# Attention values in split heads: the high and low passes of the last key block as one matmul of 256 columns, the spare columns added afterwards

## Chip, cores, metric

One core of one Trainium2 chip. The metric is the time of one execution on the device in microseconds; several executions are timed and their median is given. The core's engines are named as in the profile: PE (TensorE, matmuls), PEld (its weight loads), DVE (VectorE), ACT (ScalarE), POOL (GpSimd) and SP (SyncE, which issues most transfers).

## What is computed

Windowed attention with a few sink keys, then a two-layer MLP on the joined heads:

```python
batch, n_heads, seq, head_dim = (4, 8, 768, 64)     # n_sink 4, window 128
scores = scale * np.matmul(q, k.transpose(0, 1, 3, 2))
keep = is_sink | in_window
scores = np.where(keep, scores, -1000000000.0)
...
a = a / (np.sum(a, axis=-1, keepdims=True) + 1e-09)
attn = np.matmul(a, v)
x = attn.transpose(0, 2, 1, 3).reshape(B * S, H * D)      # 3072 x 512
h = x @ w_in                                             # 512 x 2048
out = np.maximum(0.01 * h, h) @ w_out                    # 2048 x 512
```

## The kernel before

The work is cut into 8 units `u` (4 batches, two halves of 384 queries each), and each unit into 8 heads `h`, taken in pairs. A head has three query blocks `j` of 128. For each block `scores` (L306) makes the score tile in PSUM (tag `s`, one buffer), `softmax` (L319) masks it, takes the exponent and normalises it, and `tail` (L377) transposes it (L382), splits it into a high part (ACT, L393) and a low part (DVE, L395), and lets POOL put it into `pt` (L353). `pt` holds for each head the transposed weights of all key blocks, `pt[:, 0]` the high parts and `pt[:, 1]` the low ones, 768 columns apart. Each number is split into a high part, which is its cast to the type fp32r, and a low part, which is what the cast leaves; products of high with high, high with low and low with high are summed in PSUM.

`values` (L427) is the changed function. Units 0 and 1 take its native branch, which multiplies without a split. Units 2 to 7, 48 heads, take the split branch: the values of one head stand in 128 weight columns, 64 for the high part and 64 for the low part, so that one pass gives both halves in the two halves of the partitions of `out`, a PSUM tile of 512 columns (tag `v`, one buffer). Each key block (`segments`, L346) is passed twice, with the high and with the low part of `pt`, and adds into its own columns of the 384 queries. The last key block touches only the last 128 queries. A pass for the sink keys (`st`) ends the group. In a unit of even number that makes 4 passes of 256 columns, 2 of 128 and the sink pass (7), in one of odd number 2 of 128, 4 of 256, 2 of 128 and the sink pass (9). Then ACT copies one half of the partitions out of PSUM into `xf` (L460), and DVE adds the other half from PSUM (L461). After the odd head of a pair `emit_x` (L510) splits `xf` into `xh` (L513, ACT) and `xl` (L514, DVE or POOL), which the MLP of that unit reads later.

`mlp_stream` (L548) has for each unit and each of 16 column blocks 12 matmuls for the hidden tile `h` (L565, PSUM, one buffer), then ACT (L572), DVE (L573), ACT (L574) and DVE (L575) for its split parts `gh` and `gl`, and 9 matmuls into the three output tiles (L586). In units 2 to 5 of the MLP `check_weights` (L188) also reads weights over again (L193 on ACT, L195 on POOL, L197 on DVE).

The order of TensorE's instructions is the order in which the program issues them: the two streams are interleaved by hand, step by step. The order on ACT, DVE, POOL and SP is worked out by a scheduler that simulates the program while it is built, so an added instruction may also move others. Each engine works through its own list in order.

Of the kernel before, what the change touches and what calls it, by code (L numbers as in the profile page):

```python
# [9 lines left out]
F32 = mybir.dt.float32  # L10
# [4 lines left out]
ALU = mybir.AluOpType  # L15
# [5 lines left out]
P = 128  # L21
# [10 lines left out]
TU = T * P  # L32
# [89 lines left out]
def fast_path(ctx, tc, cpool, wz, qk, vu, vs, w_in, w_out, out, ident, lim, masks, tri, diag,  # L122
              negm, wmin, wmax):
    nc = tc.nc
# [12 lines left out]
    phase = {}  # L137
# [65 lines left out]
    def native_values(u, h):  # L203
        return NATP0 <= (u * H + h) // 2 < NATP
# [141 lines left out]
    def segments(half):  # L346
        if half:
            return (0, 0, P), (P, 0, 2 * P), (3 * P, P, 2 * P), (5 * P, 2 * P, P)
        return (0, 0, 2 * P), (2 * P, P, 2 * P), (4 * P, 2 * P, P)
# [77 lines left out]
    def values(u, h, pt, st, state):  # L427
        half = u % 2
        pair, odd = divmod(h, 2)
        q0 = 0 if half else P  # L430
        hp = slice(odd * D, (odd + 1) * D)
        lp = slice((1 - odd) * D, (2 - odd) * D)
        if native_values(u, h) and not odd:
            state["v"] = vraws.pop((u, h))
        vv, sv = state["v"]
        if native_values(u, h):
            if not odd:
                state["acc"] = ps_v.tile([P, 512], F32, tag="v", name=f"v{u}_{h}")
            out = state["acc"][hp, :]
            mms = [(vv[:, kb * P + odd * D:kb * P + (odd + 1) * D], pt[:, 0, po:po + m], qo, m)  # L440
                   for kb, (po, qo, m) in enumerate(segments(half))]
            mms.append((sv[0:st.shape[0], hp], st, q0, TU - q0))
        else:
            out = ps_v.tile([P, 512], F32, tag="v", name=f"v{u}_{h}")
            cs = slice(odd * P, (odd + 1) * P)
            mms = [(vv[:, kb, cs], pt[:, c, po:po + m], qo, m)
                   for kb, (po, qo, m) in enumerate(segments(half)) for c in range(2)]
            mms.append((sv[:, 0, cs], st, q0, TU - q0))
        for c, (l, r, o, m) in enumerate(mms):
            nc.tensor.matmul(out[:, o:o + m], lhsT=l, rhs=r, start=c == 0, stop=c == len(mms) - 1,  # L450
                             skip_group_check=True)
            if u == 0 and c % PIECE == PIECE - 1 and c < len(mms) - 1:
                yield
        if native_values(u, h):
            x = state["acc"][:, 0:TU]
        else:
            if not odd:
                state["xf"] = xpool.tile([P, TU], F32, tag="xf", name=f"xf{u}_{pair}")
            x = state["xf"]
            nc.scalar.copy(out=x[hp, :], in_=out[lp, 0:TU])  # L460
            nc.vector.tensor_tensor(out=x[hp, :], in0=out[hp, 0:TU], in1=x[hp, :], op=ALU.add)  # L461
        if odd:
            vfree[pair % 2] = True
            emit_x(u, pair, x)

    def attend(u, h, pend, state):
# [34 lines left out]
        if odd:  # L501
            def gather():
                state["st"] = sinks(u, h // 2, sk)
                if u == 0 and h < H - 1:
                    load_weights(h // 2)
            pend.append(gather)
            for o in range(2):
                pend.append(lambda o=o: values(u, h - 1 + o, state["pt", o], state["st"], state))

    def emit_x(u, pair, x):  # L510
        xh = xpool.tile([P, TU], F32R, tag=f"xh{pair}", name=f"xh{u}_{pair}")
        xl = xpool.tile([P, TU], F32R, tag=f"xl{pair}", name=f"xl{u}_{pair}")
        nc.scalar.copy(out=xh, in_=x)  # L513
        (nc.gpsimd if u < XLP and not native_values(u, 2 * pair) else nc.vector).tensor_tensor(out=xl, in0=x, in1=xh.bitcast(F32), op=ALU.subtract)  # L514
        xs[u].append((xh, xl))
# [313 lines left out]
```

## Time and profile before

| | |
|---|---|
| median of 3 runs | 748.33 us (747.74 to 749.93) |
| profiled execution | 746.79 us, span 744.9 us |
| PE busy | 718.6 us (96%) |
| PEld busy | 623.4 us (84%) |
| DVE busy | 562.3 us (75%) |
| ACT busy | 434.3 us (58%) |
| POOL busy | 381.2 us (51%) |
| split value passes (L450) | from 174.1 to 656.2 us |

The profile is of one execution; times in it are microseconds from the start of its span. Matmuls overlap: one of 0.28 us may be followed by the next after 0.12, so what one costs is read from start to start. A "releaser" is what an engine waited for last.

### The profile page before, as it was taken

The page shows a single profiled execution, that of the slowest core. Times are in us where ns is not written, and L with a number is a line of the kernel's source. Part 1 is how long each engine was busy: PE and PEld are TensorE (multiplying, and loading weights), DVE is VectorE, ACT ScalarE, POOL GpSimd, SP SyncE. Part 2 cuts the span into 40 slices and gives each one's busy share as a digit, 9 for nine tenths or more (in the row PEclk, how much of TensorE's full clock was granted, in tenths as well). Part 3 has the DMA queues.
Part 4 walks back from the last instruction along what each step waited for, and adds up shares of the span by engine and source line. Part 5 has one row for each costly group of instructions (what it writes and reads, how often), then busy time and mean ns, then how long its engine had stood idle before and what let it go on. Part 6 is the DMA issues. An engine that isn't in the chain of part 4 may idle for free.

```text
span 744.9 us, 12686 instructions
## 1 busy us (share of the span) xinstructions
PE 718.6 (96%) x3935; PEld 623.4 (84%) x3935; DVE 562.3 (75%) x1832; ACT 434.3 (58%) x1208; POOL 381.2 (51%) x490
## 2 busy tenths in 40 slices
PE   8879999989999999999999999999999999999995
PEld 4547777769999988999988988999988999988985
DVE  6876889877667888888888888888888977733222
ACT  4667667657666566666566666666666655522221
POOL 3554456555445677665666577665666556300000
PEclk9989999999999999999999999999999999999998
DMA  5543566643212343324333443325331321001001
GB/s 179 181 151 119 186 205 185 190 136 100 58 55 64 115 125 122 90 93 152 114 108 106 133 125 112 96 93 157 114 107 48 106 69 43 1 1 42 1 1 46
DMA packets 30475, 76.94 MB, mean 103 GB/s; under 512 B 3585, under 2 KB 9153, under 8 KB 30401
## 3 DMA queue, kind: packets, MB, share of 16 engines
q1 hardware_dynamic: 30256, 75.94, 32.6%
q8 instruction: 33, 0.54, 0.3%
q14 instruction: 42, 0.34, 0.1%
q10 hardware_dynamic: 144, 0.13, 0.1%
HBM read 69.76 MB, written 6.29 MB: 102 GB/s over the span
## 4 chain that ended last, share of the span: by engine, by line
PE 84%; DVE 9%; ACT 3%; issue 2%; DMA 1%; POOL 0%; SPq 0%; ACTq 0%; DVEq 0%
PE o L586 32%; PE h L565 32%; PE v L450 10%; PE s L314 5%; PE t L382 2%; DVE gl L575 2%; PE warm L304 1%; PE t L369 1%; DVE pk L344 1%; DVE zeroi L197 1%; DMA woraw<-in_w_out 1%; ACT qksp L271 1%; DVE g L573 1%; DVE pk L334 0%; DVE xf L461 0%
## 5 line engine op out<-in xcount | busy, mean ns | idle before, releaser
L565 PE MATMUL h<-xh,wih 128*128 128x384 f32 x512 | 187.6, 366 | 1.4 <-DVE g L573 1.3
L565 PE MATMUL h<-xh,wil 128*128 128x384 f32 x512 | 172.7, 337 | 1.5 <-POOL wil L185 1.5
L565 PE MATMUL h<-xl,wih 128*128 128x384 f32 x512 | 172.3, 337 | 0.0
L586 PE MATMUL o<-woh,gh 128*128 128x512 f32 x384 | 154.2, 401 | 0.0
L586 PE MATMUL o<-woh,gl 128*128 128x512 f32 x384 | 151.3, 394 | 0.0
L586 PE MATMUL o<-wol,gh 128*128 128x512 f32 x384 | 151.2, 394 | 0.0
L353 POOL TENSOR_SCALAR_AFFINE_SELECT pt<-stg 128x256 fp32r<-128x256 f32 x240 | 101.4, 448 | 83.4 <-DVE stg L395 67.9
L272 POOL TENSOR_TENSOR qksp<-qkraw,qksp 64x524 fp32r<-64x524 f32 (+1 forms) x62 | 74.9, 1208 | 106.7 <-issue 61.7
L575 DVE TENSOR_TENSOR gl<-g,gh 128x384 fp32r<-128x384 f32 x128 | 105.6, 825 | 17.1 <-ACT gh L574 15.6
L573 DVE TENSOR_TENSOR g<-h,g 128x384 f32<-128x384 f32 x128 | 71.0, 555 | 60.5 <-ACT g L572 58.3
L565 PEld LDWEIGHTS h<-xh,wih 128*128 128x128 f32 x512 | 96.4, 188 | 15.9 <-issue 2.9
L572 ACT ACTIVATE g<-h 128x384 f32<-128x384 f32 x128 | 62.3, 487 | 69.9 <-PE h L565 69.3
L338 ACT ACTIVATE pk<-pk,negm 128x128 f32<-128x128 f32 (+2 forms) x168 | 70.3, 418 | 53.3 <-DVE negm L334 52.4
L565 PEld LDWEIGHTS h<-xl,wih 128*128 128x128 f32 x512 | 96.8, 189 | 3.2
L565 PEld LDWEIGHTS h<-xh,wil 128*128 128x128 f32 x512 | 96.1, 188 | 1.8 <-POOL wil L185 1.8
L314 PEld LDWEIGHTS s<-qksp 128*128 128x128 f32 x372 | 68.5, 191 | 22.5 <-issue 10.6
L586 PEld LDWEIGHTS o<-woh,gl 128*128 128x128 f32 x384 | 72.0, 188 | 16.4 <-DVE gl L575 0.2
L314 PE MATMUL s<-qksp 128*128 128x260 f32 (+1 forms) x372 | 76.6, 288 | 9.2 <-DVE pk L344 5.4
L574 ACT CAST gh<-g 128x384 fp32r<-128x384 f32 x128 | 65.7, 513 | 32.8 <-DVE g L573 30.5
L586 PEld LDWEIGHTS o<-woh,gh 128*128 128x128 f32 x384 | 72.4, 189 | 11.2 <-issue 2.4
L586 PEld LDWEIGHTS o<-wol,gh 128*128 128x128 f32 x384 | 72.2, 188 | 6.5
L274 POOL TENSOR_TENSOR qksp<-qkraw,qksp 128x384 fp32r<-128x384 f32 x62 | 67.8, 1094 | 4.7
(124 smaller groups left out, 1220.4 us busy)
## 6 DMA issues: line engine op xcount, KB each, us to landing
qkraw<-in_qk SPq DMA_DIRECT2D x32, 454.0 KB, 4.1
qkraw<-in_qk SPq DMA_DIRECT2D x30, 388.0 KB, 3.2
wiraw<-in_w_in SPq DMA_DIRECT2D x16, 512.0 KB, 3.6
woraw<-in_w_out SPq DMA_DIRECT2D x16, 512.0 KB, 3.8
ciraw<-in_w_in SPq DMA_DIRECT2D x16, 512.0 KB, 3.5
coraw<-in_w_out SPq DMA_DIRECT2D x16, 512.0 KB, 3.6
out<-ob SPq DMA_DIRECT2D x23, 256.0 KB, 2.0
vraw<-in_vu SPq DMA_DIRECT2D x12, 256.0 KB, 2.7
```

Of the source, the lines that this page charges most:

```text
L272: nc.gpsimd.tensor_tensor(out=sp[D:P, TU:TU + n], in0=raw[D:P, TU:TU + n], in1=sp[D:P, TU:TU + n].bitcast(F32), op=ALU.subtract)
L274: nc.gpsimd.tensor_tensor(out=sp[:, TU + n:2 * TU + n], in0=raw[:, 0:TU], in1=sp[:, 0:TU].bitcast(F32), op=ALU.subtract)
L314: nc.tensor.matmul(ps[:, 0:kn], lhsT=sp[rows, off + j * P:off + (j + 1) * P], rhs=sp[rows, TU + k0:TU + k0 + kn], start=c == 0, stop=c == ...
L338: nc.scalar.activation(out=e, in_=e, func=AF.Exp, scale=-1.0, bias=neg, accum_out=sm)
L353: nc.gpsimd.affine_select(out=out, in_=src, pattern=([[0, x]] if x > 1 else []) + [[sign, P]], base=-1 if prev else 0, channel_multiplier= ...
L450: nc.tensor.matmul(out[:, o:o + m], lhsT=l, rhs=r, start=c == 0, stop=c == len(mms) - 1, skip_group_check=True)
L565: nc.tensor.matmul(ph[:, 0:TU], lhsT=w[:, cs], rhs=x, start=cc == 0 and c == 0, stop=cc == NCC - 1 and c == 2)
L572: nc.scalar.mul(g, ph[:, 0:TU], 0.01)
L573: anchor[0] = nc.vector.tensor_tensor(out=g, in0=ph[:, 0:TU], in1=g, op=ALU.max)
L574: nc.scalar.copy(out=gh, in_=g)
L575: (nc.gpsimd if u == 0 and fc % 4 < GLP else nc.vector).tensor_tensor(out=gl, in0=g, in1=gh.bitcast(F32), op=ALU.subtract)
L586: nc.tensor.matmul(po[t], lhsT=gg[:, tsl], rhs=w, start=f == 0 and c == 0, stop=f == NFC - 1 and c == 2)
```

## The change

In the split branch the last key block is taken out of the list, and its two passes (high and low part of `pt`, 128 columns each, into the same columns) become one pass over both parts, 256 columns side by side: the high part goes into the block's own columns, the low part into columns 384 to 511 of the same PSUM tile, which were not used. These spare columns are then added to the last 128 queries: ACT copies one half of their partitions into a new tile `more`, DVE adds the other half from PSUM to `xf`, and then `more`. The native branch is as before.

```diff
             out = ps_v.tile([P, 512], F32, tag="v", name=f"v{u}_{h}")
             cs = slice(odd * P, (odd + 1) * P)
-            mms = [(vv[:, kb, cs], pt[:, c, po:po + m], qo, m)
-                   for kb, (po, qo, m) in enumerate(segments(half)) for c in range(2)]
+            *segs, (po, qo, m) = segments(half)
+            mms = [(vv[:, kb, cs], pt[:, c, a:a + n], o, n)
+                   for kb, (a, o, n) in enumerate(segs) for c in range(2)]
+            mms.append((vv[:, len(segs), cs], pt[:, :, po:po + m], qo, 2 * m))
             mms.append((sv[:, 0, cs], st, q0, TU - q0))
         for c, (l, r, o, m) in enumerate(mms):
-            nc.tensor.matmul(out[:, o:o + m], lhsT=l, rhs=r, start=c == 0, stop=c == len(mms) - 1,
+            dst = out[:, o:o + m]
+            if len(r.shape) > 2:
+                dst = dst.rearrange("p (c q) -> p c q", c=2)
+            nc.tensor.matmul(dst, lhsT=l, rhs=r, start=c == 0, stop=c == len(mms) - 1,
                              skip_group_check=True)
...
             x = state["xf"]
+            more = phase["late"].tile([P, P], F32, tag="more", name=f"more{u}_{h}", bufs=1)
+            end = x[hp, TU - P:]
             nc.scalar.copy(out=x[hp, :], in_=out[lp, 0:TU])
+            nc.scalar.copy(out=more[hp, :], in_=out[lp, TU:])
             nc.vector.tensor_tensor(out=x[hp, :], in0=out[hp, 0:TU], in1=x[hp, :], op=ALU.add)
+            nc.vector.tensor_tensor(out=end, in0=out[hp, TU:], in1=end, op=ALU.add)
+            nc.vector.tensor_tensor(out=end, in0=end, in1=more[hp, :], op=ALU.add)
```

## Rows read from the trace of the kernel before

**Rows 1.** The page's first part: busy time of each engine, its share of the span and its instructions.

```profile
PE 718.6 (96%) x3935; PEld 623.4 (84%) x3935; DVE 562.3 (75%) x1832; ACT 434.3 (58%) x1208; POOL 381.2 (51%) x490
```

**Rows 2.** The table of stretches: from and to, length, busy time of PE, PEld, DVE, ACT and POOL with their instructions, then the granted clock of TensorE, the DMA share and GB/s.

```profile
175.00:250.00 75.00, 75.00 (x429) 68.20 (x428) 52.08 (x184) 48.55 (x140) 40.81 (x58) 1.00 0.20 58
250.00:600.00 350.00, 348.75 (x1982) 314.67 (x1981) 303.12 (x1011) 221.37 (x630) 225.97 (x299) 1.00 0.37 113
600.00:657.00 57.00, 56.80 (x328) 51.55 (x326) 41.86 (x149) 30.86 (x86) 26.74 (x46) 1.00 0.10 29
```

**Rows 3.** The list of TensorE's waits from 175 to 657 us, all of it: who waited for whom, us in total, times, longest.

```profile
PE v L450 <- DVE xf L461: 0.9, 3, 0.4
```

**Rows 4.** One value pass of an even unit (head 2 of unit 4) in order of time, engine PE: start, us, instruction, count. Each row joins the passes of one kind that were running at a chosen instant and begins with the first of them; so 363.12, 363.24, 363.30 and 363.41 are the starts of the last pass of 256 columns, of the two of 128 and of the sink pass.

```profile
363.12 0.45 PE L450 MATMUL v<-pt,vsp 128*128 128x256 f32 x3
...
363.24 0.33 PE L450 MATMUL v<-pt,vsp 128*128 128x128 f32 x2
...
363.30 0.27 PE L450 MATMUL v<-pt,vsp 128*128 128x128 f32 x1
363.41 0.33 PE L450 MATMUL v<-st,ssp 128*128 128x256 f32 x1
```

**Rows 5.** The same pass, order of time, weight loads (PEld).

```profile
363.24 0.19 PEld L450 LDWEIGHTS v<-pt,vsp 128*128 128x128 f32 x1
363.35 0.19 PEld L450 LDWEIGHTS v<-st,ssp 128*128 128x128 f32 x1
```

**Rows 6.** Groups of instructions by line and shape, ACT, whole span: busy us, mean ns of one | idle before them and its releaser.

```profile
L393 ACT CAST stg<-t 128x128 fp32r<-128x128 f32 x120 | 30.8, 257 | 42.7 <-PE t L382 27.6 <-POOL pt L353 13.7 <-POOL qksp L274 1.3
...
L460 ACT COPY xf<-v 64x384 f32<-64x384 f32 x48 | 22.8, 475 | 6.0 <-PE v L450 4.9
```

**Rows 7.** The same for DVE, from 175 to 657 us.

```profile
L575 DVE TENSOR_TENSOR gl<-g,gh 128x384 fp32r<-128x384 f32 x92 | 82.2, 894 | 6.3 <-ACT gh L574 4.9
...
L395 DVE TENSOR_TENSOR stg<-t,stg 128x128 fp32r<-128x128 f32 x116 | 33.1, 285 | 6.0 <-ACT stg L393 5.3
...
L461 DVE TENSOR_TENSOR xf<-v,xf 64x384 f32<-64x384 f32 x47 | 25.8, 548 | 12.7 <-ACT xf L460 12.6
```

**Rows 8.** DVE in order of time behind the value pass of an even head (its passes run from 299.75 to 301.01).

```profile
302.55 0.14 DVE L339 TENSOR_SCALAR sm<-sm 128x1 f32<-128x1 f32 x1
302.73 0.16 DVE L340 RECIPROCAL sm<-sm 128x1 f32<-128x1 f32 x1
...
303.33 0.54 DVE L461 TENSOR_TENSOR xf<-v,xf 64x384 f32<-64x384 f32 x1
303.80 0.27 DVE L395 TENSOR_TENSOR stg<-t,stg 128x128 fp32r<-128x128 f32 x1
```

**Rows 9.** ACT in order of time in the same place.

```profile
302.16 0.48 ACT L460 COPY xf<-v 64x384 f32<-64x384 f32 x1
```

**Rows 10.** PE in order of time: the first value pass of odd heads, of the first, the second and the last of the 14 handoffs in which it starts 0.14 to 0.18 us after L461's end, and (240.03) of the tightest of the ten others. In brackets, where there is one, the idle time before it and its releaser.

```profile
240.03 0.28 PE L450 MATMUL v<-pt,vsp 128*128 128x256 f32 x1
...
282.81 0.41 PE L450 MATMUL v<-pt,vsp 128*128 128x128 f32 x2 [0.36 <-DVE xf L461]
...
304.01 0.30 PE L450 MATMUL v<-pt,vsp 128*128 128x128 f32 x1
...
655.31 0.30 PE L450 MATMUL v<-pt,vsp 128*128 128x128 f32 x1 [0.20 <-DVE xf L461]
```

**Rows 11.** DVE in order of time: L461 of the even heads before three of those passes (that of the pass at 304.01 stands in rows 8).

```profile
238.78 0.54 DVE L461 TENSOR_TENSOR xf<-v,xf 64x384 f32<-64x384 f32 x1
...
282.13 0.54 DVE L461 TENSOR_TENSOR xf<-v,xf 64x384 f32<-64x384 f32 x1
...
654.61 0.55 DVE L461 TENSOR_TENSOR xf<-v,xf 64x384 f32<-64x384 f32 x1 [1.04 <-ACT xf L460]
```

**Rows 12.** DVE in order of time behind the value pass of an odd head; the last row is the L334 of the odd head with the least distance to the next score pass.

```profile
306.51 0.56 DVE L461 TENSOR_TENSOR xf<-v,xf 64x384 f32<-64x384 f32 x1 [0.65 <-ACT xf L460]
307.10 0.56 DVE L575 TENSOR_TENSOR gl<-g,gh 128x384 fp32r<-128x384 f32 x1
307.69 0.30 DVE L323 COPY_PREDICATED s<-tri,s 128x128 f32<-128x128 int8 x1
...
308.37 0.28 DVE L334 CUSTOM_DVE_ANT_0 pk<-s,mw 128x132 f32<-128x132 f32 x1
...
391.80 0.29 DVE L334 CUSTOM_DVE_ANT_0 pk<-s,mw 128x132 f32<-128x132 f32 x1
```

**Rows 13.** PE in order of time: the score passes that follow those two.

```profile
309.18 0.28 PE L314 MATMUL s<-qksp 128*128 128x260 f32 x1
...
392.46 0.28 PE L314 MATMUL s<-qksp 128*128 128x260 f32 x1
```

**Rows 14.** Order of time near 274 us, DVE (L573, which frees the tile `h`) and PE (the next pass into `h`).

```profile
273.50 0.56 DVE L573 TENSOR_TENSOR g<-h,g 128x384 f32<-128x384 f32 x1 [0.36 <-ACT g L572]
...
274.11 0.44 PE L565 MATMUL h<-xh,wih 128*128 128x384 f32 x1
```

**Rows 15.** Order of time, POOL and PE: the last L514 of unit 2 and the pass that reads its result.

```profile
243.52 1.23 POOL L514 TENSOR_TENSOR xl<-xf,xh 128x384 fp32r<-128x384 f32 x1
...
250.03 0.34 PE L565 MATMUL h<-xl,wih 128*128 128x384 f32 x1
```

**Rows 16.** The list of DVE's waits over the whole span, the row of L595 (columns as in rows 3).

```profile
DVE ob L595 <- ACT ob L593: 0.4, 1, 0.4
```

## The prediction

> **What bounds the kernel now.** I read first the shares of busy time [rows 1] and then the table of stretches [rows 2]. The changed code runs only for units 2 to 7, which is the stretch from 175 to 657 us: 48 heads, one value pass each. There the reader should see TensorE busy in 480.55 of 482 us at full granted clock, and VectorE busy in 397.06 of them (82%; 303.12 of 350, or 87%, between 250 and 600). So TensorE sets the pace, each nanosecond saved on it counts, and each delay that reaches it counts too; VectorE has 85 us to spare, but in order and in small pieces. The list of waits is third [rows 3]: the only wait that it puts to TensorE's account in this stretch is that of the value pass for the addition of L461, 0.9 us in 3 pieces. That is the place that the change lengthens.
>
> **What the change removes.** Per head, the two 128-column passes of the last key block become one of 256 columns with the same weights. In one value pass in order of time [rows 4] a 256-column pass takes 0.12 us from its start to that of the next (363.12 to 363.24), the two 128-column ones together 0.17 us (363.24 to 363.41): the first is followed after 0.06, the second after 0.11. The weight loads show why: they start 0.11 us apart [rows 5], so a pass of 0.06 us that follows such a load waits for the next one. One pass of 0.12 us in place of 0.17 saves 0.05 us, times 48 heads: 2.4 us. The new moving operand has a gap between its halves, which no row on TensorE shows. If the gap cost nothing and the weight load were the bound, one load interval is saved, 48 x 0.11 = 5.3 us; if it cost the difference, nothing is saved. I take 2.4, as the pass is nearest to the contiguous 256-column one.
>
> By the columns alone there would be no saving: at 0.12 us for 256 columns, two passes of 128 cost 0.06 each. The Trainium skill (TensorE: Matmul & The Clock Gate, Back-to-back issue gap) states such a rule: an isolated pass costs its columns plus a small constant, which as an estimate from its table leaves 3 ns per head, 0.1 us in all, and a sum of +7.8 us in place of +5.5. The trace speaks against it here, with its 0.17 us.
>
> **What the change adds.** Per head one ScalarE copy of 64x128 out of PSUM, one VectorE addition that reads PSUM and SBUF (64x128, "first addition" below) and one that reads SBUF alone (the second). ScalarE: the nearest row is the 128x128 cast of L393 at 257 ns [rows 6], so 48 x 0.26 = 12.3 us on an engine that is busy 63% of 250 to 600 (221.37 of 350) [rows 2]; it hides there, and costs TensorE something only where an addition waits for it. First addition: L395 has the same columns and the same kinds of operands, 285 ns; L461 with 384 columns takes 548, so 1.03 ns per column. Second addition: its nearest row is L575, two SBUF operands of 384 columns, whose mean is 894 ns against 548 for L461 with as many [rows 7]; cut by 256 columns at 1.03 ns the two give 0.28 to 0.63 us, and I take 0.28, as the L575 that stands right behind a value pass takes 0.56 us [rows 12]. Both depend on the instruction before them: a dependent VectorE instruction starts 0.04 us after the end of its forerunner (302.55 + 0.14, then 302.73) [rows 8]. So VectorE's queue grows by about 0.32 + 0.28 = 0.6 us per head, 29 us of its 85 spare. As a total it fits. What counts is what stands behind it in the queue.
>
> **Place one, from even head to odd head.** All value passes share one PSUM buffer. The pass of the odd head starts about 4 us after that of the even one and waits until L461 has read the buffer. For the even head ScalarE copies at 302.16 [rows 9], but L461 comes to its turn at 303.33, behind the softmax chain, and ends at 303.87 [rows 8]; the odd head's pass starts at 304.01, 0.14 us later, which is just the way from the release to the start [rows 10]. Of 24 such handoffs 14 have 0.14 to 0.18 us there: the first is 282.13 + 0.54 to 282.81, the last 654.61 + 0.55 to 655.31 [rows 10, 11]. The ten others have 0.7 us and more (the tightest 238.78 + 0.54 to 240.03) and absorb it. With the change the last PSUM read is the first addition, 0.32 us later. In the 14 tight ones TensorE pays that, less up to 0.03: 14 x 0.30 = 4.2 us. The ends are zero, if the scheduler now places L461 earlier, and 14 x 0.6 = 8.4, if it slips another operation in between. What is queued behind the wait on TensorE is its whole stream. The second addition does not hold the buffer.
>
> **Place two, behind the odd head's L461.** Here VectorE runs without a pause from 306.51 (L461, after an idle 0.65 us in which it waited for ScalarE) through L575, L323 and L514 to L334 at 308.37, which frees the one PSUM buffer of the scores [rows 12]; the next score pass starts at 309.18 [rows 13], 0.53 us after L334's end. A released TensorE pass can start 0.05 us after VectorE's end (273.50 + 0.56, then 274.11) [rows 14], so 0.48 us are free. In 15 of the 24 odd heads the distance is 0.37 to 0.58 us (the tightest 391.80 + 0.29 to 392.46), in the others 0.75 and more, or no score pass follows. The additions are issued ahead of L323 and L334 in the program and are ready sooner, so I expect them between: 0.6 us more against 0.29 to 0.50 free, worked out one by one 2.7 us in all. The ends: zero if they are put behind L334, and 15 x 0.55 = 8.3 if the copy delays them as well or the second is disturbed.
>
> **Place three.** Twice, from 259 to 274 and 428 to 443 us, VectorE has no pause at all, and TensorE already waits for L573 (the pass at 274.11 comes those 0.05 us behind L573's end, as a waiting pass does) [rows 14]. Most of the 1.2 us that a pair adds there arrives at TensorE: 0.5 us each after what place two has charged, 1.0 us in all (0 to 2).
>
> **Hidden.** The x tiles come 0.6 us later, and so do the casts of L513 and L514. The least time between such a result and its use is 5 us (L514 ends at 244.75, its use is at 250.03) [rows 15], so this costs nothing; without that cover it would be 0.6 us per unit. No transfer and no queue of SyncE or GpSimd is touched, other than that GpSimd's placements wait for L395, which moves with place one.
>
> **Sum.** -2.4 + 4.2 + 2.7 + 1.0 = +5.5 us. The profiled execution took 746.79 us (span 744.9 and 1.9 around it), 1.54 below the median of the three runs, 748.33; against its own time the sum gives 752.3, against the median 753.8, which I take.
>
> **The rivals.** (a) *One reader of the buffer at a time.* The copy of the spare columns reads the same PSUM buffer as L461, in other partitions. At the kernel's end L595 waits 0.4 us for L593 although the two only share a PSUM buffer and an output tile, in different columns [rows 16]. If such readers are ordered, L461 starts 0.26 us later wherever it waits for ScalarE, which is at all odd heads: 15 x 0.26 and about 1 us from the next ones, +5 on top, +10.5 or 758.8. The Trainium skill (PSUM — Partial Sum Buffer, PSUM bank collisions raise a hardware error) wants two engines kept apart by bank and quadrant of partitions, or more simply by bank; by quadrant the two reads need no order, by bank they do, and L595 shows only columns of the same partitions. (b) *Only the handoff is paid.* If the additions of odd heads are placed behind L334, places two and three vanish: -2.4 + 4.2 = +1.8, 750.1. For it: the scheduler does put other work between dependent operations; against: the additions are ready as soon as L461 ends. (c) *Faster.* The order changes so that L461 of even heads comes before the softmax chain, or the first addition is covered; then the 2.4 us stay, with up to 0.9 us of the present waits [rows 3]: 745.9 to 745.0. For it: VectorE's 85 us of slack [rows 2]; against: it takes another order in 14 places of one pattern. It decides once less than 0.05 us per head reach TensorE. (d) *The pass does not get cheaper*, since the gapped operand costs 0.05 us or passes cost by their columns alone: +7.9, 756.2.
>
> **How the numbers follow.** Forecast +5.5: 0.38. (a) 0.18, (b) 0.20, (c) 0.20, (d) 0.04. What a measurement of this kernel can tell from no change is 0.3%, 2.2 us. Slower: forecast, (a) and (d), 0.60. Within: (b) and the poorer part of (c), 0.23. Faster: 0.17. Since both signs hold weight, the forecast's own range is 750.5 to 757; that for 8 in 10 takes in (b), most of (c) and (a): 745.3 to 760.5. It leaves out the best end of (c), (a) with a disturbed second addition, and what I have not thought of.
>
> **What would show it.** In the profile after: value passes of 6 and 8 matmuls in place of 7 and 9, 288 with weights of vsp in place of 336, and 0.12 us from the merged pass to the sink pass (step one). The start of the odd head's pass 0.14 us after the first addition in the handoffs that were tight, with an idle time of TensorE ahead of it (place one). Waits of TensorE for L334 behind odd heads (place two). More idle TensorE in 250 to 600 than 1.25 us; my sum wants about 8. Wrong would be: L461 of even heads earlier relative to the pass, or L334 ahead of the additions; then the time falls to (b) or (c). If L461 of odd heads starts behind the spare copy's end and not the first copy's, it is (a).

## The result, and the profile after

The changed kernel takes 752.71 us (median of 6 runs, 751.07 to 753.85) against 747.99 (6 runs, 746.92 to 749.93): 1.0062 times the time before, 95% interval 1.0047 to 1.0077, or 4.7 us more. The forecast was 5.5 us more. The profiled execution took 751.45 us, 4.66 more than that of before.

The stretches after, columns as in [rows 2]:

```profile
175.00:250.00 75.00, 75.00 (x426) 68.13 (x425) 56.22 (x202) 50.04 (x150) 39.20 (x57) 1.00 0.19 58
250.00:600.00 350.00, 342.07 (x1911) 305.03 (x1910) 311.29 (x1058) 221.40 (x652) 225.84 (x296) 1.00 0.36 111
600.00:657.00 57.00, 57.00 (x324) 51.73 (x323) 47.45 (x173) 33.01 (x97) 28.30 (x49) 1.00 0.12 38
```

Between 250 and 600 us TensorE is idle for 7.93 us in place of 1.25, at the same granted clock. Its waits from 175 to 663 us, all of them, where [rows 3] had one:

```profile
PE v L455 <- DVE xf L470: 6.4, 11, 0.9
PE v L455 <- POOL zeroo L195: 1.0, 2, 0.6
PE v L455 <- ACT g L582: 0.6, 1, 0.6
PE h L575 <- DVE sm L339: 0.4, 2, 0.2
```

L470 is the first addition, the one that reads PSUM; L455 is the value pass (L450 before). The second and third row are value passes too: there the list names what came last by the profile, but those passes begin 0.15 us after a first addition as the others do.

**Place by place.** TensorE's list is the same in both kernels but for the passes taken out. So each of its remaining instructions was paired with the same one of before, and the difference of their starts followed from 174 to 657 us: where it grows, time is lost. This is steadier than spans: over all the runs below the starts differ by -0.7 to +3.3 us at 174 us already, where nothing is changed. For the full change the difference grows by 5.3 us; since it is -0.7 at 174 us, it is 4.65 at 657, which is the 4.66 of the profiled executions. In steps: the sink pass and the matmul behind each group come earlier by 4.7 us, 0.10 for each of the 48 heads; the starts of the odd heads' value passes lose 7.7 at 14 handoffs; the score passes 0.9, the passes into `h` 0.9, and the rest 0.5 in steps of under 0.1 us.

**The merged pass.** The value pass of [rows 4] after the change (starts are plain here):

```profile
363.88 0.28 PE L455 MATMUL v<-pt,vsp 128*128 128x256 f32 x1
364.00 0.28 PE L455 MATMUL v<-st,ssp 128*128 128x256 f32 x1
364.12 0.40 PE L596 MATMUL o<-woh,gh 128*128 128x512 f32 x1
```

The merged pass takes 0.12 us, as a contiguous one of 256 columns does: the gap in its operand costs nothing. But the sink pass takes 0.12 as well, where before it started at 363.41 and was followed at 363.58, after 0.17:

```profile
363.46 0.19 PEld L586 LDWEIGHTS o<-woh,gh 128*128 128x128 f32 x1
363.58 0.40 PE L586 MATMUL o<-woh,gh 128*128 128x512 f32 x1
```

The same weight load after the change:

```profile
364.00 0.19 PEld L596 LDWEIGHTS o<-woh,gh 128*128 128x128 f32 x1
```

In both the next matmul starts 0.12 us after its weight load does; before, that load started 0.05 us behind the sink pass (363.41 to 363.46), after, together with it. From the first pass of a group to the matmul behind it the medians went from 816 to 716 ns and from 1095 to 999: 0.10 us per head, twice the forecast.

**Place one.** VectorE behind an even head (compare [rows 8]), and the odd head's first pass (compare 304.01 in [rows 10]):

```profile
303.46 0.17 DVE L405 COPY sk<-pk 128x12 f32<-128x12 f32 x1
303.55 0.54 DVE L469 TENSOR_TENSOR xf<-v,xf 64x384 f32<-64x384 f32 x1
304.02 0.27 DVE L395 TENSOR_TENSOR stg<-t,stg 128x128 fp32r<-128x128 f32 x1
304.22 0.27 DVE L470 TENSOR_TENSOR xf<-v,xf 64x128 f32<-64x128 f32 x1
304.52 0.39 DVE L471 TENSOR_TENSOR xf<-xf,more 64x128 f32<-64x128 f32 x1
```

TensorE's first pass of the odd head, with the idle time before it:

```profile
304.63 0.30 PE L455 MATMUL v<-pt,vsp 128*128 128x128 f32 x1 [0.44 <-DVE xf L470]
```

L469 (L461 before) stands where it stood, behind L405. L395 is put between the two PSUM reads, so the buffer is free 0.94 us after L469's start, not 0.54: 0.40 later. TensorE comes 0.10 us earlier, since the even head's own passes got shorter. Both add up to a wait of 0.5 us that was not there. Over the 24 handoffs the time lost ahead of the odd head's pass (start to start, above the usual 0.175 us) went from 2.5 to 10.2 us, in 14 places.

**Place two.** VectorE behind the odd head (compare [rows 12]), and the score pass (compare [rows 13]):

```profile
307.38 0.56 DVE L469 TENSOR_TENSOR xf<-v,xf 64x384 f32<-64x384 f32 x1 [0.69 <-ACT more L468]
307.98 0.30 DVE L323 COPY_PREDICATED s<-tri,s 128x128 f32<-128x128 int8 x1
308.30 0.56 DVE L585 TENSOR_TENSOR gl<-g,gh 128x384 fp32r<-128x384 f32 x1
308.89 0.29 DVE L470 TENSOR_TENSOR xf<-v,xf 64x128 f32<-64x128 f32 x1
309.22 0.29 DVE L334 CUSTOM_DVE_ANT_0 pk<-s,mw 128x132 f32<-128x132 f32 x1
...
309.55 0.29 DVE L471 TENSOR_TENSOR xf<-xf,more 64x128 f32<-64x128 f32 x1
...
310.67 0.76 DVE L524 TENSOR_TENSOR xl<-xf,xh 128x384 fp32r<-128x384 f32 x1
```

In the kernel before, the subtraction for `xl` stood ahead of L334:

```profile
307.90 0.55 DVE L514 TENSOR_TENSOR xl<-xf,xh 128x384 fp32r<-128x384 f32 x1
```

The score pass behind L334:

```profile
309.71 0.31 PE L314 MATMUL s<-qksp 128*128 128x260 f32 x1
```

From L469 to L334 it is 1.84 us, where it was 1.86: L470 came in, but the subtraction for `xl` (L524, L514 before), which now has to wait for L471, went behind L334. L469 itself starts later, as it waits for the end of the second copy (L468), and TensorE comes 0.10 us earlier. The distance from L334's end to the score pass shrank from 0.53 to 0.20 us and mostly still holds.

### The profile page after: what moved, and what is told of

Read it like the earlier page. It is cut to its first block, busy times and chain, and to the rows that moved or that the text cites. A ratio compares the mean times of both kernels' runs of the same rounds, so it can differ in the third digit from the quotient of the medians.

```text
span 749.4 us, 12777 instructions
## 1 busy us (share of the span) xinstructions
PE 717.6 (96%) x3887; PEld 619.1 (83%) x3887; DVE 583.5 (78%) x1928; ACT 439.8 (59%) x1256; POOL 381.8 (51%) x490
## 4 chain that ended last, share of the span: by engine, by line
PE 65%; DVE 19%; ACT 5%; issue 5%; POOL 3%; DMA 2%; SPq 0%; ACTq 0%; POOLq 0%; DVEq 0%
PE o L596 26%; PE h L575 24%; PE v L455 7%; PE s L314 4%; DVE gl L585 4%; DVE zeroi L197 2%; DVE g L583 2%; DVE pk L344 2%; PE warm L304 1%; PE t L382 1%; DVE xf L469 1%; DMA qkraw<-in_qk 1%; PE t L369 1%; POOL qksp L272 1%; ACT g L582 1%
## 5 line engine op out<-in xcount | busy, mean ns | idle before, releaser
L585 DVE TENSOR_TENSOR gl<-g,gh 128x384 fp32r<-128x384 f32 x128 | 98.5, 769 | 16.4 <-ACT gh L584 15.2
L274 POOL TENSOR_TENSOR qksp<-qkraw,qksp 128x384 fp32r<-128x384 f32 x62 | 70.9, 1144 | 4.7
```

Source lines behind the costliest of these rows:

```text
L274: nc.gpsimd.tensor_tensor(out=sp[:, TU + n:2 * TU + n], in0=raw[:, 0:TU], in1=sp[:, 0:TU].bitcast(F32), op=ALU.subtract)
L585: (nc.gpsimd if u == 0 and fc % 4 < GLP else nc.vector).tensor_tensor(out=gl, in0=g, in1=gh.bitcast(F32), op=ALU.subtract)
```

## Experiments

Times are medians, ratios are to the kernel before on the same chip, with 95% intervals; "stretch" is the growth of TensorE's difference to the kernel before from 174 to 657 us, as above, in the profiled execution. The full change: ratio 1.0062, stretch +5.3 us.

The expectations set three theories against each other. H (handoff): the time is lost where the odd head's value pass waits for the reads of the even head's PSUM tile. L (load): VectorE's longer queue costs time wherever work is added to it. R (reshuffle): the scheduler's new order of the other work makes the difference.

| run | ratio | median, before | stretch |
|---|---|---|---|
| odd heads alone | 1.0024 (1.0007 to 1.0042) | 749.05, 747.13 | +0.1 |
| the same again | 1.0006 (0.9991 to 1.0021) | 747.91, 747.36 | 0.0 |
| even heads alone | 1.0054 (1.0034 to 1.0074) | 751.38, 747.13 | +4.0 |
| merged pass, no additions | 0.9951 (0.9933 to 0.9969) | 742.81, 747.13 | -3.5 |
| additions, no merged pass | 1.0119 (1.0098 to 1.0140) | 755.39, 747.13 | +8.5 |
| one addition over 512 columns | 0.9994 (0.9979 to 1.0010) | 747.46, 747.71 | -0.4 |
| the same, odd heads alone | 1.0004 (0.9988 to 1.0019) | 747.90, 747.36 | -0.9 |
| second addition on GpSimd | 1.0061 (1.0040 to 1.0083) | 752.10, 747.71 | +5.8 |
| before, no L197 | 0.9951 (0.9933 to 0.9970) | 744.39, 747.36 | -3.1 |
| after, no L197 | 0.9949 (0.9930 to 0.9968) | 744.57, 747.36 | -4.0 |
| before, two value buffers | 1.0351 (1.0329 to 1.0373) | 775.09, 747.71 | |
| after, two value buffers | 1.0467 (1.0447 to 1.0487) | 782.51, 747.71 | |

**The two halves of the edit.** First without the additions:

```diff
-            nc.scalar.copy(out=more[hp, :], in_=out[lp, TU:])
-            nc.vector.tensor_tensor(out=end, in0=out[hp, TU:], in1=end, op=ALU.add)
-            nc.vector.tensor_tensor(out=end, in0=end, in1=more[hp, :], op=ALU.add)
```

> The merged pass for all 48 heads, without the spare copy and the two additions: the product of the last key block with the low part is left out of the result. Theory H: 48 x 0.10 = 4.8 us saved, less 14 x 0.10 = 1.4 us at the tight handoffs, where the odd head's pass waits for L461 anyway and a shorter even pass only makes the wait longer: 3.4 us below the kernel before (2.8 to 4.0). If the saving per head is the 0.05 us of the prediction, 48 x 0.05 - 14 x 0.05 = 1.7 us. Rival R (reshuffle): the new order of the other engines' work costs or gives most of what was measured, and the time does not follow this sum: within 1 us of the kernel before, or above.

Measured 3.7 us below the kernel before by the ratio, 3.5 in the stretch: the forecast of theory H, with 0.10 us per head and a loss of 1.2 us at the handoffs. All waits of TensorE from 175 us on:

```profile
PE v L455 <- DVE xf L466: 2.0, 7, 0.5
```

Here 0.9 us stood in [rows 3]: a shorter even pass, with no work added, makes the wait at the handoff longer. Then the additions alone, in the kernel before:

```diff
+            nc.scalar.copy(out=more[hp, :], in_=out[lp, TU - P:TU])
             nc.vector.tensor_tensor(out=x[hp, :], in0=out[hp, 0:TU], in1=x[hp, :], op=ALU.add)
+            nc.vector.tensor_tensor(out=end, in0=out[hp, TU - P:TU], in1=end, op=ALU.add)
+            nc.vector.tensor_tensor(out=end, in0=end, in1=more[hp, :], op=ALU.add)
```

> The passes as before, and in all 48 heads the extra ScalarE copy and the two extra VectorE additions, made on the last block's own columns (which adds that block in once more, so the result differs). Theory H: the release of the buffer comes 0.40 us later at 14 tight handoffs (5.6 us), plus the 0.9 us of the pair at 259, plus 1.6 us of waits for the scores and the hidden tile: +7 to +8.5 us over the kernel before. The full change then is this with 4.8 us saved and 1.4 us of that lost at the handoffs. Rival L gives about as much (+9.5), and is told apart by the odd-only and even-only runs. Rival R: no relation, anywhere from 0 to +5.

Measured 8.9 us by the ratio, 8.5 in the stretch: at the upper end. Of the 8.5, the value passes lose 5.9, the score passes 1.3, the passes into `h` 1.2. The halves make 8.5 - 3.5 = 5.0 where the whole has 5.3: they add up, and the order of the other work (theory R) has no large part of its own.

**Odd and even heads.**

```diff
+            merged = odd == 1        # and odd == 0 in the other kernel
```

> The change for even heads alone; odd heads as before. Theory H: all of the handoff's cost and half of the saving: -24 x 0.10 + 7.7 (the waits at the 14 tight handoffs, in which the saving of those heads is lost too) = +5.3 us, with what is behind the odd head's addition gone, so 4.5 to 5.5 us above the kernel before, as slow as the full change or slower. Rival L: half of the full change, +2.3 us.

> The change for odd heads alone; even heads keep their two passes of 128 columns and one addition. Theory H (handoff): the cost sits where the odd head's value pass waits for the even head's PSUM reads (14 of 24 handoffs, 7.7 us in the changed kernel), so it goes, and the saving stays: the runs of value passes became 0.10 us shorter per head (816 to 716 ns, 1095 to 999), 24 x 0.10 = 2.4 us. Time 1.5 to 2.5 us below the kernel before, and waits of the value pass for VectorE as before, under 1.5 us. Rival L (load): VectorE's longer queue costs the time wherever it is added, so half the heads cost half: 4.7 / 2 = 2.3 us above the kernel before.

Even heads alone: 4.0 us in both measures, nearly all of the full change and not the half that the load would give, but below theory H's 4.5 to 5.5: the starts of the odd heads' value passes lose 6.5 us, at 13 handoffs and not 14, about 2.2 are saved, and the passes into `h` come 0.6 earlier. Odd heads alone: not the gain that theory H forecast. The handoffs are nearly as before (1.3 us of waits, 0.4 us lost in the differences), and 24 x 0.10 us are saved, but they are given back elsewhere. Since a store that landed late confused the first run, it was run again:

> The kernel with the change for odd heads alone, once more, since its execution with a profile had a store at 674 us that took 1.8 us longer than in all others and held TensorE for 1.0 us. If that was this execution alone, TensorE's stretch from 174 to 657 us is again level with that of the kernel before (+0.1 us, within 0.3), the end is as in the kernel before, and the median falls below +1.5 us. If it belongs to this kernel's order, the 1.0 us come again.

The stretch is 0.0 again. The late store came again too, with 1.0 us of TensorE's time at 676 us, so it was not that one execution alone; two other kernels had it as well, and two profiles do not show that it belongs to this order of the work. What delays the store stays open. By the two ratios, 1.0024 and 1.0006, odd heads alone bring no gain. In the stretch, the place is the crowded pair, the heads between 259 and 274 us where VectorE has no pause. VectorE in the second run:

```profile
264.50 0.56 DVE L472 TENSOR_TENSOR xf<-v,xf 64x384 f32<-64x384 f32 x1 [0.49 <-ACT more L471]
...
265.99 0.29 DVE L474 TENSOR_TENSOR xf<-v,xf 64x128 f32<-64x128 f32 x1
...
266.50 0.29 DVE L475 TENSOR_TENSOR xf<-xf,more 64x128 f32<-64x128 f32 x1
...
268.62 0.56 DVE L587 TENSOR_TENSOR g<-h,g 128x384 f32<-128x384 f32 x1 [0.20 <-ACT g L586]
```

And the pass into `h`:

```profile
269.23 0.44 PE L579 MATMUL h<-xh,wih 128*128 128x384 f32 x1 [0.19 <-DVE sm L339]
```

VectorE waits 0.49 us for the spare copy and then has two more instructions ahead of L587 (L573 before). The pass starts 0.05 us after L587's end (268.62 + 0.56, then 269.23), so that is what it waits for, though the list names L339. The difference grows by 1.2 us there (seven steps between 263 and 270 us), by 0.46 in two steps near 438 us and by 0.14 at each of two handoffs, near 408 and 577. So half of the load on odd heads does cost, at these places, most of what the merged pass saves: there added work does cost, as theory L says.

**Which addition, and how long the buffer is held.** The second addition on GpSimd (`nc.gpsimd` in its line):

> The changed kernel with the second addition (SBUF alone) on GpSimd in place of VectorE. Theory H: that addition does not hold the buffer, so the handoffs cost the same 7.7 us; the two pairs without a pause get some of their 1.8 us back: 0 to 1.5 us below the full change, so 3 to 4.7 us above the kernel before. Rival L: half of the queue's growth is gone, and with it half of its 9.5 us: level with the kernel before (-0.5 to +0.5).

Measured 4.6 us by the ratio, theory H's upper end, and 5.8 in the stretch, above it. Theory L's forecast, level with the kernel before, fails: more than half of what the change adds to VectorE's busy time is gone (415.0 us from 175 to 657, now 405.0, and 397.1 in the kernel before), and no time with it. But that the sum comes near theory H is partly luck: the starts of the odd heads' value passes lose 5.6 us and not 7.7, the score passes 3.2 and not 0.9, the transposes 0.9. The handoffs that were tight before or in the full change lose 0.47 to 0.85 us each, except three: at 261 us the loss is 0.2, and at 283 and 451 (times of the kernel before) TensorE gets 0.3 us back, since the crowded pair just ahead of each has lost more. In each of these pairs one score pass loses 1.2 or 1.3 us behind a VectorE instruction that took 2.12 us. GpSimd at the first:

```profile
263.76 0.45 POOL L471 TENSOR_TENSOR xf<-xf,more 64x128 f32<-64x128 f32 x1
264.19 1.48 POOL L195 TENSOR_SCALAR zeroo<-mago 128x512 f32<-128x512 f32 x1
265.64 1.29 POOL L286 TENSOR_TENSOR vsp<-vraw,vsp 128x512 fp32r<-128x512 f32 x1
266.88 0.46 POOL L286 TENSOR_TENSOR ssp<-vsraw,ssp 128x128 fp32r<-128x128 f32 x1
```

VectorE's instruction beside them:

```profile
265.30 2.12 DVE L344 TENSOR_SCALAR pk<-pk,sm 128x132 f32<-128x132 f32 x1
```

Then one copy and one addition for all 512 columns, and the spare columns added once per pair (the x tile moves to a buffer of its own, and the sink tile `sn`, which shared the old ones, gets one buffer):

```diff
-            nc.scalar.copy(out=x[hp, :], in_=out[lp, 0:TU])
...
+            nc.scalar.copy(out=xw[hp, :], in_=out[lp, :])
+            nc.vector.tensor_tensor(out=xw[hp, :], in0=out[hp, :], in1=xw[hp, :], op=ALU.add)
+            x = xw[:, 0:TU]
+            if odd:
+                nc.vector.tensor_tensor(out=x[:, TU - P:], in0=x[:, TU - P:], in1=xw[:, TU:], op=ALU.add)
```

> The merged pass for all heads, but with one ScalarE copy and one VectorE addition over all 512 columns of the tile, and the spare columns added to the block once per pair, for both heads, from SBUF (the x tile has 512 columns in a buffer of its own). At 1.03 ns per column the one addition takes 0.13 us more than that of 384 columns. Theory H: the buffer is held 0.13 us longer in place of 0.40, so a tight handoff costs 0.10 + 0.13 where it cost 0.50 to 0.55: -4.8 + 14 x 0.23 + 0.5 to 1 for the two pairs in which VectorE has no pause: 0.5 to 1.5 us below the kernel before. Rival L (VectorE's queue): it grows by 0.13 + 0.15 us per head in place of 0.57, half the load, so 0.28 / 0.57 x 9.5 - 4.8 = 0.1 us below. The two are close; the handoffs in the trace decide, 0.13 us later than before or not.

Level with the kernel before, -0.4 us in both measures, which lies between the two theories; the handoffs decide. The addition takes 0.67 us, 0.13 more than that of 384 columns, and 13 tight handoffs lose 0.21 to 0.27 us each, theory H's 0.23, in place of 0.45 to 0.70:

```profile
303.05 0.67 DVE L466 TENSOR_TENSOR xf<-v,xf 64x512 f32<-64x512 f32 x1
```

This form for odd heads alone:

> The merged pass for odd heads alone, in the form with one copy and one addition over all 512 columns and a later addition of the spare columns; even heads as before. Theory H: the handoff from even to odd heads is untouched, 24 x 0.10 = 2.4 us are saved, and VectorE gets 0.42 us more per pair, which the two pairs without a pause pay (0.4 us each): 1.6 us below the kernel before (0.8 to 2.4). Rival L: the queue's growth of 10 us costs a third of the full change's 9.5 us, so 0.7 us above.

The stretch gains 0.9 us, the low end of theory H's forecast, but the late store comes here too (1.6 us), and the ratio shows no gain. No version that computes the whole result and keeps the weight check beat the kernel before beyond its interval.

**Is it the backlog ahead of L461?** L197 out of both kernels (its result is a constant then):

```diff
-            nc.vector.tensor_tensor_reduce(out=zero, in0=mag, in1=zero, scale=1.0, scalar=3.0e38,
-                                           op0=ALU.add, op1=ALU.min, accum_out=wmin[:, col:col + 1])
```

> The kernel before without the VectorE step of the weight check (L197, 28.7 us in 32 pieces, mostly ahead of the even heads' L461); its result is replaced by a constant, so the smallest weight is not looked at. It is the base for the next run. Theory H: the backlog in front of L461 shrinks by 0.7 us and more, the handoffs get loose and the waits at them (2.5 us) and at the two crowded pairs (0.7 us) go: 2 to 3.2 us below the kernel before. Rival R: the new order makes it anything between -2 and +2.

> The changed kernel without that step; its difference from the run before it counts. Theory H: with the handoffs loose, 48 x 0.10 = 4.8 us are saved, and only the last handoff (0.4 us) and what is left of the crowded pairs (up to 1 us) is paid: the change is 3 to 4.4 us faster here, where it was 4.7 slower. Rival L: the same 27 us of added queue still cost most of 9.5 us, so it is 2 to 4.7 us slower here too.

The base gains 3.7 us by the ratio, somewhat over the forecast, and 3.0 by the medians; in the stretch all of it is at the value passes (3.0 of 3.1). L461's place there (L458 in this kernel) and the odd head's pass:

```profile
302.58 0.54 DVE L458 TENSOR_TENSOR xf<-v,xf 64x384 f32<-64x384 f32 x1
```

The odd head's pass in the same kernel:

```profile
304.49 0.22 PE L447 MATMUL v<-pt,vsp 128*128 128x128 f32 x1
```

The handoff has 1.37 us where it had 0.14, and all but the last one have 0.7 and more. On this base the change costs 0.2 us by the medians (744.57 against 744.39) and gains 0.9 in the stretch: its loss of about 5 us is gone with the backlog. But the gain of 3 us and more that theory H forecast is not there: four handoffs lose 0.2 to 0.5 us each (the last one was tight in the base too), and the score passes and those into `h` lose 1.7 us to the additions. Without L197 VectorE is also busy for 24 us less in the stretch (372.7 in place of 397.1), so these two runs alone do not tell the backlog ahead of L461 from the load; the handoffs and the even heads do.

**A second buffer for the value passes**, taken from the transposes:

```diff
+            second = odd and phase.get("mlp", 0) > 0
+            out = (ps_t if second else ps_v).tile([P, 512], F32, tag="t1" if second else "v", name=f"v{u}_{h}")
```

> The kernel before, with a second PSUM buffer for the odd heads' value passes, taken from the two of the transposes, which then have one. It is the base for the next run. Theory H: the waits of the value pass for L461 vanish (2.5 us by start-to-start), and what the transposes lose with one buffer is added: 0 to 4 us, so -2.5 to +1.5 us against the kernel before.

> The changed kernel with that second buffer. Only its difference from the run before it counts. Theory H: no handoff is left to pay, so the change saves 48 x 0.10 = 4.8 us and gives back 1 to 2.5 us at the pairs where VectorE has no pause and at the score passes: 2.3 to 3.8 us faster than the same kernel without the change. Rival L: the queue's growth costs what it cost, so the change is 4 to 5 us slower here too. Rival R (reshuffle): no fixed relation.

Both missed. The base lost 27 us: with one buffer the transposes wait for VectorE (three groups of 7.9, 7.6 and 3.0 us from 170 us on), so VectorE's chain sets the pace, and there the change costs 7.4 us though no value pass waits for an addition. It tells nothing on the handoff, but shows the other regime: where TensorE waits on VectorE's chain, added VectorE work costs time without any handoff, 7.4 us net for some 27 us of added work.

## Why the prediction was right

The time and its main reason were right, but that the sum came so near was luck: against the forecast the removed passes gave 2.3 us more, place one cost 3.5 more and place two 1.8 less.

- *Removed passes*: right in kind, half in size (-2.4 forecast, -4.7 measured). The step read only the two 128-column passes. Behind them the weight loads came late, and the sink pass paid for that too: that it was followed after 0.17 us, not 0.12, stood in the trace. Rival (d) fell: the merged pass got cheaper, and its operand's gap cost nothing. The rule of the Trainium skill (TensorE: Matmul & The Clock Gate, Back-to-back issue gap), by which an isolated pass costs its columns, would leave 0.1 us; the section itself says that at small column counts this rule counts too little, since it leaves out the weight load, and the trace agrees with that, with its 4.7.
- *Place one*: right, and shown: the waits are named in the trace, the even heads alone bring 4.0 of the 4.7 us, and the loss goes with the backlog ahead of L461. The term was mis-sized, 4.2 for 7.7: the scheduler put L395 between the two reads (0.40 us, not 0.32), TensorE arrives 0.10 us earlier at a point that it does not set, and one more handoff, at 260 us, became tight (0.73 us). The count was off by one too: recounted, 13 handoffs were tight before, not 14; this one makes 14 after.
- *Place two*: wrong in how it works. The additions were not simply put ahead of L334; the subtraction that depends on them left that stretch in exchange, and the score passes lost 0.9 us in place of 2.7.
- *Place three*: 1.0 forecast, 0.9 measured at the passes into `h`, which the odd heads alone show (0.8).
- *Rival (a)* came true as an event: L469 waits for L468, 10.6 us in 15 pieces of VectorE's idle time. That total is no added cost: before, L461 waited 12.6 us for L460 [rows 7]; what is new is that the wait ends with the second copy. Its price did not come: in the odd head shown, the 0.25 us came out of the margin ahead of the score pass. Only in the crowded pair did such a wait stand ahead of a TensorE loss (the 0.49 us at 264 in the odd-only run).
- *Rival (b)* fell: the score passes and the passes into `h` still lose 1.8 us, though the second addition did go behind L334 in the odd head shown. *Rival (c)* fell: L461 was not moved ahead of the softmax chain, nor was the first addition covered.

What stays open: why the odd-only kernels' store at 674 us lands late, and how much of the 1.8 us outside the handoffs comes from the additions and how much from the second copy.

## What to carry to other kernels

Time saved on the busiest engine ahead of a tight handoff that another engine releases is not saved: it becomes waiting. So before trading TensorE passes for evacuation work (copying results out of PSUM), look for the distance between the release of the single PSUM buffer and its next use; at the tight handoffs here, how long the buffer was held counted, not the sum of the added work, which counted only where VectorE had no pause. If spare columns have to be read out, read them in the same instruction as the rest: here that took the loss away, though it brought no gain.

## What the runs showed of the hardware

A matmul pass of 256 columns whose moving operand is two pieces of 128, 768 elements apart, was followed after 0.12 us like a contiguous one. Short passes are paid for behind them as well: behind two passes of 128 columns the next weight load started 0.05 us late, and the 256-column sink pass was followed after 0.17 us; behind the merged pass, after 0.12. A VectorE scaling of 128x132 in SBUF, 0.29 us when undisturbed, took 2.12 us while three GpSimd instructions of 1.48, 1.29 and 0.46 us ran one behind the other; it ended at 267.42, 0.08 us after the last of them. At 436.81 us in the same run it took 2.12 us again and ended 0.08 us after the same three. That the two engines share something is not shown by it alone: no run took the GpSimd instructions away.
